# The list schedule of a transformer block's end: one shared interface for VectorE and GpSimd, subtractions dealt to either engine, new keys

## The chip, the cores and the metric

The kernel runs on one core of a Trainium2 chip. The metric is device time in microseconds for one launch. The kernel before takes 968.0 us (median of three runs, 967.63 to 968.37). Engines are named as in the profile: PE (TensorE matmuls), PEld (its weight loads), DVE (VectorE), ACT (ScalarE), POOL (GpSimd), SP (SyncE, which here issues the DMAs).

## The reference

One block with adaptive layer norm, sequence 2048, width 512, all in float32:

```python
mod = (_silu(c) @ w_mod).reshape(c.shape[0], 6, 1, -1)          # sa, ca, ga, sb, cb, gb
h = _layernorm(x) * (1 + ca) + sa
x = x + ga * A(h, wqkv, wo)      # 32 heads of 16, window of 256 keys, softmax, then @ wo
h = _layernorm(x) * (1 + cb) + sb
x = x + gb * ((_silu(h @ w1) * (h @ w3)) @ w2)                  # inner width 1792
```

## The kernel before, in words

**Arithmetic.** A float32 product is made of three PE products of halves: each operand is split into a high part (rounded to the PE's fp32r, by ACT) and a low part (operand minus high part, one TENSOR_TENSOR on DVE or POOL). So every operand costs an ACT copy and a subtraction with two inputs in SBUF; these subtractions are what the change is about.

**Stages.** First projections and layer norm 1. Then 32 units of attention, one per four heads and quarter of the sequence ("block" b = 0 to 3, 512 rows): scores (L485 for the row maxima, L752 for the probabilities), maxima on DVE (L494), masks on DVE (L760, L772), exponentials on ACT (L765, L767), products with the values into the bank `po` (L720), a copy `os` (L814) stored to `o_dr[b]` (L817). The rows of q and k go through `ringq` and `ringk` by DMA (L457, L459). The last units also hold nothing but their own work and what the end puts between.

**The end.** What follows the attention is one program of some thousand operations, and its first part is laid between the last units of attention. For each block: `o_sums` loads the softmax sums (L1065, tile `wqr` for the first 24 heads of a block, `mT` for the last 8), takes reciprocals on DVE (L1069) and stores them to `r_dr`; `o_part` loads four quarters k of the attention's output (L1089) and the spread reciprocals (L1084), multiplies them (L1101), and splits the result: high part on ACT (L1093), low part (L1096), into tiles `o` (blocks 0, 2, 3) or `x1b` (block 1). `o_proj` multiplies with `wo` (L1113, 48 matmuls a block, 12 per tile of 128 rows); `add_stats` adds the residual on DVE with a row sum (L982) and squares on ACT (L990); `ln_rstd` makes 1/sqrt on POOL (L1004) between two small DVE operations (L1001, L1007). `ln2` applies layer norm 2 to blocks 0 and 1 on ACT (L1233), transposes on PE (L1247), scales on ACT (L1251, tiles t0 to t3), and forms the operands of one level of Strassen's scheme: sums and differences (`sub`, L1264, tiles t1 to t5) and splits (`cut`, L1270 on ACT and L1272, tiles b000 to b611: operand, half k, part). `half_rows` does the layer norm of blocks 2 and 3 for later (L1299 on ACT, L1308 on PE, L1312). The FFN follows: 14 steps of 14 products `up` (L1375, six matmuls each), sums on DVE (L1406), gates, and 8 products `down` (L1468). Its weights are loaded (L1171, L1214) and split (`split`: L966 on ACT, L967 on POOL).

**What sets the order.** The operations of the end are recorded with engine, duration, priority (`key`), the tiles they read and write. `Sched.deal` walks in time: for each engine it takes the first ready operation in order of key that can start when the engine is free, and issues the earliest over all engines. The attention's remaining operations stand in `fixed` at given times and are merged in; they go first at equal time. Every engine runs its queue in this order, so an operation that waits for a tile holds all that stand behind it on its engine. Durations of the plan: a subtraction 0.85 on DVE or 1.29 on POOL, engines independent of each other. Which engine makes a product or subtraction is written out: in `K["by"]` for `o_part`, as an argument in `ln2` (`cut(B11, h11, "DVE")`, `sub(t3, h22, h12, "POOL")`), POOL for the weights. `K` also has the keys.

## Time and profile before

| | |
|---|---|
| median of three runs | 968.0 us (967.63 to 968.37) |
| the profiled execution's own time | 967.35 us |
| its span, first to last instruction | 965.6 us |
| mean granted clock | 0.988 |
| busy: PE, DVE, ACT, POOL | 921.7, 672.0, 524.8, 544.1 us |
| last product of the attention ends (L720) | 471.4 us after the span's start |
| last matmul of `o_proj` ends (L1113) | 532.9 us |

The span is 1.75 us shorter than that execution's own time, and the execution is 0.65 us under the median; the prediction makes its sum on the span and adds both. In the lines quoted below, a row of a timeline has start and duration in us, engine, line and operation, output<-inputs with shapes, how many are merged in the row, and in brackets the idle time before it and what ended it. A row of a table by stretches has the stretch, its length, busy time (and number of instructions) of PE, PEld, DVE, ACT and POOL, the granted clock of PE, the DMA engines' share and GB/s. A row of waits has who waited for whom, the total in us, how often, and the longest.

### The profile page before, as it was taken

How to read it: one execution, taken by the hardware profiler on the slowest of the kernel's cores; microseconds unless marked ns; L12 is line 12 of the kernel's file. 1: busy time of each engine (PE TensorE's matmuls, PEld its weight loads, DVE VectorE, ACT ScalarE, POOL GpSimd, SP SyncE). 2: the span in 40 equal slices, each digit the busy share in tenths (PEclk: the TensorE clock that was granted, in tenths of full speed). 3: DMA queues.
4: the chain of work that ended last, by engine and by line, in shares of the span. 5: the costliest groups of instructions: out<-in, count | busy, mean ns of one | idle time of the engine just before them, and what ended most of it. 6: DMA issues, size and time to landing. Idle time of an engine off the chain costs nothing.

```text
span 965.6 us, 16735 instructions
## 1 busy us (share of the span) xinstructions
PE 921.7 (95%) x5330; PEld 708.9 (73%) x5330; DVE 672.0 (70%) x1864; ACT 524.8 (54%) x1031; POOL 544.1 (56%) x691
## 2 busy tenths in 40 slices
PE   5999999999999999978987999999999999999998
PEld 2678677777777777755665878888888888888886
DVE  7575689898898989876568555675569645565455
ACT  3333677787877777764677654333455334433330
POOL 5221465676656665643665689986657446443420
PEclk9999999999999999998998999999999999999999
DMA  9532466656665665566870668654254512322002
GB/s 307 174 87 46 105 186 163 153 149 163 183 170 139 163 160 149 138 181 183 247 218 1 206 222 312 215 184 162 77 166 149 182 42 95 98 65 92 25 22 87
DMA packets 125020, 141.62 MB, mean 147 GB/s; under 512 B 60034, under 2 KB 72834, under 8 KB 124932
## 3 DMA queue, kind: packets, MB, share of 16 engines
q1 hardware_dynamic: 124212, 139.51, 49.3%
q10 hardware_dynamic: 720, 1.05, 0.3%
q8 instruction: 42, 0.69, 0.3%
q14 instruction: 46, 0.38, 0.1%
HBM read 85.72 MB, written 34.61 MB: 125 GB/s over the span
## 4 chain that ended last, share of the span: by engine, by line
PE 82%; DVE 7%; ACT 3%; DMA 3%; issue 3%; SPq 1%; POOL 1%; DVEq 0%; POOLq 0%; ACTq 0%
PE mx L1375 12%; PE st L1375 12%; PE pj L438 9%; PE st L752 8%; PE mx L485 8%; PE po L720 8%; PE st L1468 7%; PE mx L1468 7%; PE pj L1375 4%; PE st L652 2%; PE pj L1468 2%; PE st L1113 1%; PE mx L1113 1%; DVE junk L494 1%; DMA wo<-wsum 1%
## 5 line engine op out<-in xcount | busy, mean ns | idle before, releaser
L494 DVE CUSTOM_DVE_ANT_0 junk<-mx,mskq 128x320 bf16<-128x320 f32 (+4 forms) x512 | 223.0, 465 | 37.9 <-PE mx L485 37.1
L967 POOL TENSOR_TENSOR w<-w,w 128x512 fp32r<-128x512 f32 (+2 forms) x56 | 106.8, 1924 | 117.5 <-ACT w L966 99.0
L485 PE MATMUL mx<-ringk,ringq 96*128 96x320 f32 (+4 forms) x512 | 153.8, 324 | 5.5 <-DMA ringq<-qk 3.0
L752 PE MATMUL st<-ringq,ringk 98*128 98x256 f32 (+1 forms) x528 | 141.4, 336 | 7.1 <-DVE st L772 3.1
L779 POOL TENSOR_SCALAR_AFFINE_SELECT pt<-pt 128x256 f32<-128x256 f32 x224 | 92.4, 412 | 88.3 <-ACT pt L767 80.7
L438 PE MATMUL pj<-hT,wq 128*128 128x512 f32 x384 | 132.3, 402 | 1.8 <-ACT wq L423 1.0
L485 PEld LDWEIGHTS mx<-ringk,ringq 96*128 96x128 f32 x512 | 97.8, 192 | 44.5 <-DVE mt L494 21.4
L767 ACT ACTIVATE pt<-st 128x512 f32<-128x512 f32 (+1 forms) x198 | 115.8, 587 | 25.9 <-DVE st L760 7.7
L752 PEld LDWEIGHTS st<-ringq,ringk 98*128 98x128 f32 x528 | 91.1, 193 | 22.0 <-ACT pt L767 5.4
L720 PE MATMUL po<-pt,vS 128*17 128x384 f32 (+2 forms) x1408 | 92.5, 392 | 2.8 <-ACT pt L767 1.5
L438 PEld LDWEIGHTS pj<-hT,wq 128*128 128x128 f32 x384 | 68.3, 191 | 10.2 <-ACT wq L423 1.4
L1375 PE MATMUL mx<-b,w 128*128 128x512 f32 x264 | 68.2, 397 | 6.0 <-ACT t L1409 5.7
L1406 DVE TENSOR_TENSOR t<-mx,t 128x512 f32<-128x512 f32 x48 | 33.0, 689 | 45.3 <-PE mx L1375 22.6
L1406 DVE TENSOR_TENSOR t<-st,t 128x512 f32<-128x512 f32 x48 | 33.1, 690 | 44.7 <-PE st L1375 25.0
L720 PEld LDWEIGHTS po<-pt,vS 128*17 128x17 f32 x1408 | 34.8, 98 | 39.4 <-issue 19.9
L1375 PEld LDWEIGHTS mx<-b,w 128*128 128x128 f32 x264 | 50.1, 191 | 17.2 <-ACT t L1409 6.0
L1446 ACT ACTIVATE wq<-g 128x512 fp32r<-128x512 f32 x28 | 17.7, 631 | 81.6 <-DVE g L1402 33.6
L772 DVE COPY_PREDICATED st<-later,st 128x256 f32<-128x256 uint8 x112 | 47.4, 423 | 18.7 <-PE st L752 16.2
L1375 PE MATMUL st<-b,w 128*128 128x512 f32 x240 | 60.3, 390 | 0.0
L794 POOL TENSOR_SCALAR_AFFINE_SELECT sm<-sm 128x256 f32<-128x256 f32 x109 | 42.6, 409 | 28.7 <-ACT sm L784 27.7
L760 DVE TENSOR_TENSOR st<-st,mskr 128x256 f32<-128x256 f32 x125 | 53.6, 429 | 7.0 <-PE st L752 5.8
L451 POOL TENSOR_TENSOR qk<-qkr,qk 128x512 fp32r<-128x512 f32 x32 | 42.2, 1320 | 25.8 <-ACT qk L447 25.8
(262 smaller groups left out, 2020.7 us busy)
## 6 DMA issues: line engine op xcount, KB each, us to landing
ringk<-qk SPq DMA_DIRECT2D x96, 128.0 KB
ringq<-qk SPq DMA_DIRECT2D x192, 64.0 KB
o_dr<-os SPq DMA_DIRECT2D x32, 256.0 KB
w<-wsum SPq DMA_DIRECT2D x14, 512.0 KB
w<-w2g SPq DMA_DIRECT2D x14, 512.0 KB
jb<-in_w SPq DMA_DIRECT2D x24, 256.0 KB
wraw<-in_w SPq DMA_DIRECT2D x7, 768.0 KB
w<-wraw SPq DMA_DIRECT2D x14, 384.0 KB
```

The costliest lines, as they stand in the source:

```text
L438: nc.tensor.matmul(v["ps"], WQ[g][w][:, n // 3], hTp(i, n // 3, b * BT, BT), start=(n == 0), stop=(n == 3 * KC - 1))
L485: nc.tensor.matmul(v[i][:, :n], both_queries(a, gs), keys(NS, a, (gs + 1) * HP - n, n), start=True, stop=True)
L494: nc.vector.tensor_tensor_reduce(out=junk[:, :n], in0=v[i][:, :n], in1=mskq[:, WK - n:], scale=1.0, scalar=-3e38, op0=ALU.add, op1=ALU.max ...
L720: nc.tensor.matmul(po[32 * i:32 * i + DH + 1, qb * P:(qb + nq) * P], vS[:, kb, 4 * g + i], pts[i // 2][:, i % 2, c0:c0 + nq], start=first, ...
L752: nc.tensor.matmul(o, keys(NM, a, kb * P, P), queries(a, q, n), start=q == lo, stop=not plus and q + n == hi, skip_group_check=True)
L760: nc.vector.tensor_tensor(out=ps, in0=ps, in1=mskk[:, p:p + 1].to_broadcast([P, 2, P]), op=ALU.add)
L767: nc.scalar.activation(held[u, j, a][:, :, :n], v[j, a, 0].rearrange("p (h q) k -> p h q k", h=2)[:, :, :n], AF.Exp, scale=SCALE)
L779: nc.gpsimd.affine_select(out=pt[:, :, 2 * m], in_=pt[:, :, 0], **w)
L967: sch.op(eng, lambda: on_eng(eng).tensor_tensor(out=lo(), in0=src(), in1=hi().bitcast(F32), op=ALU.subtract), 0.06 + 0.0024 * n if eng == ...
L1375: nc.tensor.matmul(ps(bk), WT[s, n][w][:, col], BB[t, k][r], start=start and c == 0, stop=stop and c == 5, skip_group_check=True)
L1406: return nc.vector.tensor_add(o, x, y)
L1468: nc.tensor.matmul(ps(bk), tiles[hk + (h,)][:, i * P:(i + 1) * P], w2_of(last, y, f), start=(m == 0), stop=(m == 5))
```

## The change

`Sched.op` gets a flag `port`, and `deal` a time `port` until which the one interface is taken: an operation with two inputs in SBUF on DVE or POOL starts only when it is free. POOL's operations of the attention (`fixed`) take it too, DVE's do not. The low part in `o_part` and its multiplication, `sub` and `cut` in `ln2`, and weight splits with a key under `w0` + 13 are recorded for either engine (`both`); whichever would end earlier gets them, at 0.72 (DVE) or 1.32 (POOL) for 512 columns. All keys in `K` are new, and so is `n`, the number of quarters that must be there before the first product of a block's tile (1, 1, 2, 1 before, 2, 2, 3, 1 now). What is computed stays the same. The core of the diff:

```diff
-    def op(self, eng, fn, occ, key, reads=(), writes=(), lat=None, mode=0):
+    def op(self, eng, fn, occ, key, reads=(), writes=(), lat=None, mode=0, port=False):
+
+
         o = Op()
-        o.eng, o.fn, o.occ, o.key, o.mode = eng, fn, occ, key, mode
+        o.both = occ if isinstance(occ, dict) else None
+        if o.both:
+            eng, port, occ = "DVE", True, occ["DVE"]
+        o.eng, o.fn, o.occ, o.key, o.mode, o.port = eng, fn, occ, key, mode, port
...
-            insort(ready[o.eng], (o.key, o.seq, o))
+            for e in ("DVE", "POOL") if o.both else (o.eng,):
+                insort(ready[e], (o.key, o.seq, o))
...
-                    s = o.est
+                    s = max(o.est, port) if o.port else o.est
+                    if o.both:
+                        a, z = (max(s, free[x]) + o.both[x] for x in (e, "POOL" if e == "DVE" else "DVE"))
+                        if z < a:
+                            continue
...
+                if e == "POOL":
+                    port = max(port, free[e])
...
+            if o.both:
+                o.eng, o.occ = e, o.both[e]
+                o.lat = o.occ + HOP[e]
...
+            if o.port:
+                port = max(port, free[o.eng])
+            order.append((lambda fn=o.fn, e=o.eng: fn(e)) if o.both else o.fn)
...
-BY = ((("POOL", "POOL"),) * 3 + (("DVE", "DVE"),), (("POOL", "POOL"),) * 3 + (("DVE", "DVE"),),
-      (("POOL", "DVE"),) * 3 + (("DVE", "DVE"),), (("POOL", "POOL"),) * 4)
 K = dict(be=(('DVE', 'DVE'), ('DVE', 'POOL'), ('DVE', 'POOL'), ('POOL', 'POOL'), ('POOL', 'DVE'),
-         ('POOL', 'DVE'), ('DVE', 'DVE')), hr=0.109, de=7.098, wo=-0.159, x1=5.764, xb=-29.382,
-         xl=0.241, os=-0.129, ol=(-15.316, -4.484, -6.572, 4.956), pl=(3.999, 1.87, -4.828,
-         102.62), pe=(0.982, -5.962, 56.258, 232.622), o=(1.381, 8.497, 20.124, -0.531), n=(1, 1,
-         2, 1), w0=62.113, l2=0.424, f=1.543, fl=40.897, by=((('POOL', 'POOL'), ('DVE', 'DVE'),
-         ('DVE', 'POOL'), ('DVE', 'DVE')), (('DVE', 'DVE'), ('DVE', 'POOL'), ('DVE', 'DVE'),
-         ('DVE', 'POOL')), (('POOL', 'POOL'), ('POOL', 'DVE'), ('DVE', 'POOL'), ('POOL', 'DVE')),
-         (('POOL', 'DVE'), ('DVE', 'POOL'), ('DVE', 'POOL'), ('DVE', 'POOL'))), w=0.559, dn=1.412,
-         ds=0.003, l3=-0.027)
+         ('POOL', 'DVE'), ('DVE', 'DVE')), hr=-16.49, de=-4.33, wo=-4.756, x1=14.729, xb=-20.73, xl=16.783,
+         os=-10.171, ol=(-2.159, 0.83, 2.928, 0.264), pl=(8.637, 0.137, -19.926, 113.617), pe=(-7.191, -13.987,
+         57.285, 244.957), o=(-12.234, 1.729, 12.09, -3.422), n=(2, 2, 3, 1), w0=61.143, l2=4.34, f=14.693,
+         fl=45.503, w=10.173, dn=1.848, ds=0.034, l3=-21.35)
...
+    EITHER, ANYT = dict(DVE=0.72, POOL=1.32), K["w0"] + 13
...
+        if key < ANYT:
+            sch.op(None, lambda e: on_eng(e).tensor_tensor(
+                out=lo(), in0=src(), in1=hi().bitcast(F32), op=ALU.subtract),
+                   dict(DVE=0.08 + 0.00125 * n, POOL=0.06 + 0.0025 * n), key, kl + kh, kl)
+            return
         sch.op(eng, lambda: on_eng(eng).tensor_tensor(
             out=lo(), in0=src(), in1=hi().bitcast(F32), op=ALU.subtract),
-               0.06 + 0.0024 * n if eng == "POOL" else 0.85, key, kl + kh, kl)
+               0.06 + 0.0024 * n if eng == "POOL" else 0.85, key, kl + kh, kl, port=True)
...
-        sch.op("POOL", root, 1.0, key, sq, ["rs" + tag])
+        sch.op("POOL", root, 1.0, key, sq, ["rs" + tag], port=True)
...
-        by, minus = K["by"][b][k]
-        sch.op(by, lambda: on_eng(by).tensor_tensor(out=v["ot"], in0=v["ot"], in1=v["rt"], op=ALU.mult),
-               SPAN[by], key + 0.4, [on, rn], [on])
+        sch.op(None, lambda e: on_eng(e).tensor_tensor(out=v["ot"], in0=v["ot"], in1=v["rt"], op=ALU.mult),
+               EITHER, key + 0.4, [on, rn], [on])
         sch.op("ACT", hi, act(512) + 0.1, key + 0.4, [on], [(on_, 0, k)])
-        sch.op(minus, lo, SPAN[minus], key + 0.4, [on, (on_, 0, k)], [(on_, 1, k)])
+        sch.op(None, lo, EITHER, key + 0.4, [on, (on_, 0, k)], [(on_, 1, k)])
...
-                def go():
+                def go(e):
                     if o[0] not in tiles:
                         fresh(o[0], o[1], F32, (P, BT), "fp")
-                    (nc.gpsimd if eng == "POOL" else nc.vector).tensor_tensor(
-                        out=tiles[o[0]], in0=tiles[a[0]], in1=tiles[b[0]], op=ALU.subtract)
-                sch.op(eng, go, 1.29 if eng == "POOL" else 0.85, key, [a[1], b[1]], [o[1]])
+                    on_eng(e).tensor_tensor(out=tiles[o[0]], in0=tiles[a[0]], in1=tiles[b[0]], op=ALU.subtract)
+                sch.op(None, go, EITHER, key, [a[1], b[1]], [o[1]])
...
-                sch.op(eng, lambda: (nc.gpsimd if eng == "POOL" else nc.vector).tensor_tensor(
+                sch.op(None, lambda e: on_eng(e).tensor_tensor(
                     out=BB[m, k][1], in0=tiles[src[0]], in1=BB[m, k][0].bitcast(F32),
-                    op=ALU.subtract), 1.29 if eng == "POOL" else 0.85, key, [src[1], hi], [lo])
+                    op=ALU.subtract), EITHER, key, [src[1], hi], [lo])
```

Line numbers in the new kernel differ: `o_sums` loads at L1084 and takes reciprocals at L1088, `o_part` multiplies at L1117 and subtracts at L1113, the row sums are at L1001, `sub` and `cut` at L1280 and L1287, the weights' subtraction at L982 (either engine) or L986 (POOL), 1/sqrt at L1023.

**First place: the queue of SP, and DVE behind it, in the last units of attention** (about 418 us before, 53 us ahead of the attention's last product). `wqr<-o_dr` are loads of the softmax sums, `x1a<-in_x` of the residual, `wo<-wog` of the output weights, `ringq`, `ringk` the rows for the next unit's scores. SP before:

```order
L457 DMA ringk<-qk_7040 32x2x512
L1065 DMA wqr<-o_dr_71 96x1x128
L1050 DMA x1a<-in_x 128x512 x4
L1044 DMA wo_7148<-wog 128x512 x4
L1065 DMA wqr<-o_dr_72 96x1x128
L459 DMA ringq<-qk_7109 16x16x64 x2
L457 DMA ringk<-qk_7109 32x2x512
```

and now:

```order
L469 DMA ringk<-qk_7040 32x2x512
L1084 DMA wqr<-o_dr_71 96x1x128
L1084 DMA wqr<-o_dr_72 96x1x128
L1084 DMA wqr<-o_dr_73 96x1x128
L1084 DMA wqr<-o_dr_74 96x1x128
L1106 DMA wq_7160<-o_dr_71 128x1x512
L1069 DMA x1a<-in_x 128x512 x2
L1063 DMA wo_7148<-wog 128x512 x4
L1069 DMA x1a<-in_x 128x512 x2
L471 DMA ringq<-qk_7109 16x16x64 x2
L469 DMA ringk<-qk_7109 32x2x512
```

Two more loads of sums and one quarter of the attention's output now stand ahead of the rows. On DVE the four reciprocals of these sums stood singly, in four places of the last units; now one row holds them all, at the first of those places, ahead of a mask:

```order
L772 TENSOR_TENSOR st<-st,mskr 128x256
L1088 RECIPROCAL wqr<-wqr 96x128 x4
L784 COPY_PREDICATED st<-later,st 128x2x128
```

Later on DVE, where POOL had them or where they stood after the attention's maxima, three multiplications (L1117) and three subtractions (L1113) of block 0 now stand between the maxima of the last two units.

**Second place: DVE at the end of the attention** (about 461 to 472 us before). The masks L760 (now L772) are the last that the attention needs. Before:

```order
L1101 TENSOR_TENSOR qk_7615<-qk_7615,qk_7584 128x512
L1101 TENSOR_TENSOR wq_7419<-wq_7419,wq_7541 128x512
L760 TENSOR_TENSOR st<-st,mskr 128x2x128
L1096 TENSOR_TENSOR o_7150<-wq_7419,o_7149 128x512
L1069 RECIPROCAL mT<-mT 32x128
L1101 TENSOR_TENSOR wq_7716<-wq_7716,wq_7668 128x512
L760 TENSOR_TENSOR st<-st,mskr 128x2x128
L982 ISA x1a,nmB_7772<-pj,x1a 128x512
```

and now:

```order
L1088 RECIPROCAL mT<-mT 32x128
L772 TENSOR_TENSOR st<-st,mskr 128x2x128 x2
L1088 RECIPROCAL mT<-mT 32x128
L982 TENSOR_TENSOR wo_7148<-wo_7148,wo_7147 128x512
L1117 TENSOR_TENSOR wq_7428<-wq_7428,wq_7550 128x512
L1117 TENSOR_TENSOR qkr<-qkr,qk_7652 128x512
L1117 TENSOR_TENSOR qk_7722<-qk_7722,qk_7663 128x512
L1113 TENSOR_TENSOR o_7150<-wq_7428,o_7149 128x512
L1117 TENSOR_TENSOR wq_7732<-wq_7732,wq_7677 128x512
L1001 ISA x1a,nmB_7832<-pj,x1a 128x512
```

The two masks now stand together, with no multiplication between them. The fourth quarter of block 0 (`wq_7428`, before `wq_7419`) was multiplied and split ahead of the last mask and is now done behind it.

**Third place: the operands of the FFN** (about 504 to 526 us before). POOL before, from the weights' splits to the 1/sqrt of block 3:

```order
L967 TENSOR_TENSOR w21_7829<-w21_7829,w20_7828 128x512
L1264 TENSOR_TENSOR t4_8103<-t1_8076,t2_8089 128x512
L1272 TENSOR_TENSOR b201_7805<-t1_8076,b200_7804 128x512
L1272 TENSOR_TENSOR b501_7817<-t4_8103,b500_7816 128x512
L1264 TENSOR_TENSOR t4_8155<-t1_8140,t2_8147 128x512
L1272 TENSOR_TENSOR b211_7807<-t1_8140,b210_7806 128x512
L1272 TENSOR_TENSOR b511_7819<-t4_8155,b510_7818 128x512
L1096 TENSOR_TENSOR o1_7150<-wq01_7958,o0_7149 128x512
L1096 TENSOR_TENSOR o1_7150<-qk1_7886,o0_7149 128x512
L1096 TENSOR_TENSOR o1_7150<-wq00_7898,o0_7149 128x512
L1004 TENSOR_TENSOR rsB2_8049<-sqB2_8048,nhalf_65 128x4
```

Of these, POOL now has the weights' split and the 1/sqrt alone. On DVE there now stands, in one run from the first difference (t4 of half 0) to the second half's:

```order
L1280 TENSOR_TENSOR t4_8128<-t1_8106,t2_8114 128x512
L1280 TENSOR_TENSOR t2_8114<-t2_8114,t0_7999 128x512
L1280 TENSOR_TENSOR t5_8141<-t1_8106,t2_8114 128x512
L1287 TENSOR_TENSOR b501_7801<-t4_8128,b500_7800 128x512
L1287 TENSOR_TENSOR b101_7785<-t3_8126,b100_7784 128x512
L1287 TENSOR_TENSOR b401_7797<-t5_8141,b400_7796 128x512
L1287 TENSOR_TENSOR b301_7793<-t2_8114,b300_7792 128x512
L1280 TENSOR_TENSOR t5_8141<-t3_8126,t5_8141 128x512
L1287 TENSOR_TENSOR b201_7789<-t1_8106,b200_7788 128x512
L1287 TENSOR_TENSOR b011_7783<-t0_8150,b010_7782 128x512
L1287 TENSOR_TENSOR b601_7805<-t5_8141,b600_7804 128x512
L1280 TENSOR_TENSOR t4_8174<-t1_8169,t2_8164 128x512
```

Then t2, t5 and b111 follow, the last operand of the second product `up`: 15 subtractions on DVE with nothing else between. Before, DVE's queue held 13 operations from b101 to b111, two of them of another kind (an L1096 and an L982), while POOL had the six L1264 and L1272 shown above beside it. On PE one product changed its place there: the third product `up` (operand b4) now stands ahead of the last 36 matmuls of `o_proj`, where before the second was the last ahead of them. In the rest of the FFN the same products stand in nearly the same order, the products `down` behind the whole of the next 14 products `up` instead of among the last of them.

25 lines of the change are left out of this document (12 added, 13 removed).

## The prediction

> **What bounds the kernel now.** I read the page's busy times first, then the stretches of 20 us, then what PE waited for in the stretch where it is not full.
>
> ```profile
> span 965.6 us, 16735 instructions
> PE 921.7 (95%) x5330; PEld 708.9 (73%) x5330; DVE 672.0 (70%) x1864; ACT 524.8 (54%) x1031; POOL 544.1 (56%) x691
> ...
> 420.00:440.00 20.00, 14.49 (x93) 10.03 (x93) 12.54 (x42) 10.41 (x23) 10.35 (x15) 0.83 0.77 219
> 480.00:500.00 20.00, 16.73 (x74) 12.98 (x72) 15.87 (x29) 13.95 (x25) 16.66 (x10) 1.00 0.94 286
> 500.00:520.00 20.00, 12.74 (x58) 9.99 (x57) 15.18 (x20) 16.55 (x31) 11.35 (x8) 0.89 0.06 24
> 520.00:540.00 20.00, 18.98 (x78) 15.55 (x79) 10.55 (x24) 12.33 (x24) 5.74 (x5) 0.86 0.30 93
> 540.00:560.00 20.00, 20.00 (x96) 16.37 (x95) 13.84 (x15) 16.27 (x26) 19.05 (x14) 1.00 0.55 176
> sum 160.00, PE 137.31 PEld 103.51 DVE 101.90 ACT 100.54 POOL 97.96; mean PE 17.16 PEld 12.94 DVE 12.74 ACT 12.57 POOL 12.24
> ...
> PE mx L1375 <- ACT t L1409: 5.7, 1, 5.7
> PE st L752 <- DVE st L772: 2.9, 3, 2.0
> PE mx L485 <- DVE mt L494: 1.5, 1, 1.5
> PE mx L1308 <- ACT e L1312: 1.0, 1, 1.0
> ```
>
> PE is full 95% of the span. From 420 to 580 us (the sum row is of those eight stretches) it is busy 137.3 of 160 us, in several of them at a granted clock of 0.83 to 0.89; from 540 us on it is full but for one wait of 1.0. So the kernel is PE from end to end with 22.7 us of holes where attention hands over to the FFN, and the change, which moves only work of that handover, can win or lose there alone. PE's work is the same before and after. Below, T is the end of the attention's last L720 (471.4, the row of 470.98 under A).
>
> **The change part by part.**
>
> *D, the operands of the FFN: what the change is best at.* The rows are DVE's, POOL's, ACT's and PE's of the stretch of the longest hole.
>
> ```profile
> 506.00 0.69 DVE L1272 TENSOR_TENSOR b<-t,b 128x512 fp32r<-128x512 f32 x1 [4.57 <-ACT b L1270]
> 506.61 3.50 DVE L1264 TENSOR_TENSOR t<-t,t 128x512 f32<-128x512 f32 x2
> 513.34 3.13 DVE L1272 TENSOR_TENSOR b<-t,b 128x512 fp32r<-128x512 f32 x2
> 516.39 3.42 DVE L1264 TENSOR_TENSOR t<-t,t 128x512 f32<-128x512 f32 x2
> 519.74 4.04 DVE L1272 TENSOR_TENSOR b<-t,b 128x512 fp32r<-128x512 f32 x3
> ...
> 504.71 1.28 POOL L1264 TENSOR_TENSOR t<-t,t 128x512 f32<-128x512 f32 x1 [5.80 <-ACT t L1251]
> 514.19 3.40 POOL L1272 TENSOR_TENSOR b<-t,b 128x512 fp32r<-128x512 f32 x2
> 517.56 1.71 POOL L1096 TENSOR_TENSOR o<-wq,o 128x512 fp32r<-128x512 f32 x1
> ...
> 503.21 1.43 ACT L1251 ACTIVATE t<-st,modc 128x512 f32<-128x512 f32 x2
> 505.33 1.68 ACT L1270 ACTIVATE b<-t 128x512 fp32r<-128x512 f32 x3
> ...
> 521.01 2.93 PE L1375 MATMUL mx<-b,w 128*128 128x512 f32 x6 [5.68 <-ACT t L1409]
> ```
>
> A subtraction alone steps by 0.61 on DVE (506.00 to 506.61) and takes 1.28 on POOL. Beside each other both slow down: DVE 1.56 to 1.71 (3.13 and 3.42 for two), POOL 1.70. The two therefore yield a pair per 1.70 us, 0.85 an operation, while DVE alone yields one per 0.61, and each step of a chain is 1.1 us shorter on it. From ACT's first t1 (503.21) to the second product `up` (521.01) the stretch takes 17.8 us now. In the new order that product needs 15 subtractions on DVE (the third place shown above): 15 x 0.61 = 9.2. ACT then is the slower: ahead of b110's high part its queue has seven L1251 of 0.72, eight L1270 of 0.56 (rows above), one square, counted like an L1233 of 0.80, and one L1093 of 0.62 (both in the rows of term B): 5.0 + 4.5 + 0.8 + 0.6 = 10.9, then b111 itself and a handover, 0.9. That is 11.8, **-6.0**. Bounds: a chain that goes to and fro between ACT and DVE instead of streaming could add 3; the DVE rate alone would give 9.8, so -3 to -8.
>
> The Trainium skill ("SBUF — State Buffer", section "SBUF: two separate sides") calls this pair of ports an exclusive lock, held for a whole instruction while the other engine stands still. By that a pair would cost 0.69 + 1.28 = 1.97 and not the 1.70 of the rows; the measured rate decides, and with POOL's share gone the new stretch is the same by either. The rule also speaks against the change: it leaves POOL three weight splits (w11 and two of w21) just where DVE now does all the rest, and by a lock each would hold DVE for its whole length; ACT is busy there beyond them (term B), so the sum would not change.
>
> *A, the last units of attention.*
>
> ```profile
> 418.51 0.87 SPq L1065 DMA_DIRECT2D wqr<-o_dr  x1
> 424.78 1.34 SPq L459 DMA_DIRECT2D ringq<-qk  x2
> 428.07 1.69 SPq L1065 DMA_DIRECT2D wqr<-o_dr  x2
> 430.04 0.57 SPq L1089 DMA_DIRECT2D qkr<-o_dr  x1
> ...
> 425.48 5.17 DMA ringq<-qk
> ...
> 421.18 0.95 DVE L1069 RECIPROCAL wqr<-wqr 96x128 f32<-96x128 f32 x1 [1.71 <-DMA wqr<-o_dr]
> 469.47 0.69 DVE L1101 TENSOR_TENSOR wq<-wq,wq 128x512 f32<-128x512 f32 x1 [0.92 <-POOL o L1096]
> 470.08 0.43 DVE L760 TENSOR_TENSOR st<-st,mskr 128x256 f32<-128x256 f32 x1
> 470.98 0.41 PE L720 MATMUL po<-pt,vS 128*17 128x128 f32 x8 [1.46 <-ACT pt L767]
> ```
>
> Three more reciprocals ahead of the mask: it comes 3 x 0.9 = 2.7 later, and PE waits for it already (the L772 wait of 2.0). The rows for the next scores leave SP later by the two more loads (1.7) and the quarter of output (0.6), 2.3, with 256 KB more ahead of them in flight, 1.2 at the 219 GB/s of that stretch: up to 3.5. The two delays run side by side: +3.0. Against them: three reciprocals are gone from DVE later (2.7), six multiplications and subtractions of 0.61 are added among the maxima (3.7), where DVE was late for PE by 1.5 once (the L494 wait): +0.4. At the end the two last masks no longer stand behind a multiplication that waits for its tiles, so the wait of 1.46 goes, and of the earlier waits for masks about 1.0; three multiplications of block 1 now stand ahead of a mask: +0.9; -1.5 together. **A = +1.9**, bounds -1 (all of the first delay absorbed by what waits for the rows anyway) to +4 (every addition on the path).
>
> *B, from T to the first t1.* Loads and copies of the first weights, and the first applications of layer norm 2:
>
> ```profile
> 474.46 0.54 SPq L1171 DMA_DIRECT2D w<-wraw  x1
> 478.83 0.54 SPq L1214 DMA_DIRECT2D w<-w2g  x1
> ...
> 480.24 0.85 ACT L966 ACTIVATE w<-w 128x768 fp32r<-128x768 f32 x1 [0.46 <-DMA w<-wraw]
> 484.66 0.80 ACT L1233 ACTIVATE wqr<-x1a,nbB,rsB 128x512 f32<-128x512 f32 x1
> 507.62 0.62 ACT L1093 ACTIVATE o<-qkr 128x512 fp32r<-128x512 f32 x1
> ```
>
> PE has 117 matmuls of `o_proj` left at T, now as before (27 of block 0's 48 stand ahead of it in both orders); at 0.227 (the chain's row of 36 in 8.17, under E) that is 26.6. Two waits join it. The fourth quarter of block 0 now stands behind the last mask: a reciprocal of 0.9 and five operations of 0.61 from T - 1.0, done at T + 2.9, while PE wants it at T + 0.7: 2.2. And ACT takes all four weight copies and both of w2 ahead of the first L1233; a weight's load took 5.8 from issue to copy (474.46 to 480.24), w2's is issued at T + 7.4, later by the one delayed store, so ACT is through at about T + 16 and the fourth applied tile comes 4 to 5 later, where PE has come to want them at T + 18: 2. With 0.9 for eight transposes, at half a matmul each, PE is at T + 31.7 and ACT, after two high parts, begins t1 at T + 33.6. Before it was 503.21, T + 31.8. **B = +1.8**, bounds -2 (both waits hidden) to +4 (loads 2 us later still). DVE's last row sum of block 1, late today behind POOL's splits, comes earlier, which the queue of ACT hides.
>
> *E, the first products.* Two rows of the chain of waits; `x36` and `x6` are matmuls:
>
> ```profile
> 476.40 8.17 PE st L1113 x36
> ...
> 533.45 1.39 PE st L1375 x6
> ```
>
> From 521.01 to the end of the third product (533.45 + 1.39) PE takes 13.8, part of it at half the clock after the hole. In the new order the same three groups hold two products (1.4 to 2.9 each), 36 matmuls (8.2) and transposes (0.4): 13.1. **E = -0.7**, bounds 1 either way. *F, the later wait of 1.0*: the transposes L1308 that waited for e now all stand ahead of the first products `down`, so I take **-1.0**, bounds -1 and 0. The rest of the FFN I cost at nothing: PE covers it, POOL is at 19.05 of 20 and yet nobody waits for it; should its cover fail, a split of 128x1024 late by its own length would cost about 2.5.
>
> Sum: 1.9 + 1.8 - 6.0 - 0.7 - 1.0 = -4.0. The span becomes 961.6, with the 1.75 around it 963.35; that execution is 0.65 under the median, so **964.0 us**.
>
> **The rivals.** *Larger gain.* A and B come to nothing, because the delays at the first place fall into waits that PE has anyway and the weights land in time: -7.7 and up to 1 more, **about 959.5**. For it: 22.7 us of holes, and DVE only 12.54 of 20 busy at 420. Against it: PE waited for just those two things. *No change.* The gain of D is real but the FFN's first stage was to wait anyway, or A and B are at their upper parts, +6: -1.6 or less, **about 967.5**. *Slower.* DVE's queue becomes the attention's brake: an operation that waits for a DMA holds masks and maxima behind it, in three places (the multiplications between the maxima, the one ahead of the third last mask, the reciprocal `mT` ahead of block 0's last row sum). Price: 3 to 5 us each, as the loads of 5.17 and the wait of 1.71 above show. It decides once two of the three come late: 2 x 3.5 beyond A, B and D as above gives +3, **about 971.5**. For it: the DMA share of 0.77 to 0.94 in these stretches. Against it: the loads are issued earlier too. *The change does nothing*: excluded for the moves, which the new order shows; possible for the effect, counted with no change.
>
> **How the numbers follow.** A difference under 0.2% (1.9 us) can't be told from no change by this measurement. Chances: forecast (-1.9 to -6) 0.37, larger gain 0.21, no change 0.20, slower 0.22. So faster 0.58, same 0.20, slower 0.22. The time is that of the forecast, 964.0; its own range by the bounds of the terms is 961 to 967. The range for 8 in 10 takes in the larger gain with D at its bound (956.5) and the slower case (971.5).
>
> **What would show it.** D right: DVE's L1280 and L1287 at steps of 0.6 to 0.7 with POOL idle beside them, and 11 to 13 us from t1 to the second product `up`. A: the end of L720 at 472 to 474. B: a wait of about 2 for block 0's fourth quarter and one on the applied tiles. E, F: o_proj's end at about 529 and no wait of PE after it. The forecast is wrong if the attention ends after 476, if DVE's subtractions still take 1.5 or more each, or if PE waits for weights in the FFN.

## The result, and the profile after

The change makes the kernel slower: 976.7 us (median of nine runs, 972.8 to 982.9) against 968.4 us (967.6 to 971.8) for the kernel before on the same chip, ratio 1.0074 with a 95% interval of 1.0056 to 1.0092. The same kernel timed once more gave 1.0067 [1.0041, 1.0093]. The forecast was 964.0, its range 956.5 to 971.5.

The page of the kernel after, and what PE waited for from 420 us to the end. The profiled execution is its longest, so its 15.5 us over the span before overstate the loss.

```profile
span 981.1 us, 16716 instructions
PE 928.9 (95%) x5330; PEld 711.7 (73%) x5330; DVE 691.8 (71%) x1885; ACT 528.6 (54%) x1031; POOL 502.7 (51%) x670
...
PE st L764 <- DVE st L784: 4.8, 2, 4.5
PE mx L497 <- DVE mt L506: 3.9, 2, 2.1
PE st L1390 <- ACT t L1424: 3.9, 1, 3.9
PE mx L497 <- DMA r_dr<-wqr: 3.0, 1, 3.0
PE st L1390 <- DVE x1a L1488: 2.5, 2, 1.8
PE st L1129 <- ACT st L1009: 1.8, 1, 1.8
PE mx L1390 <- DVE t L1421: 1.8, 1, 1.8
```

The first, second and fourth rows lie in the attention, the third and sixth in the turn from attention to FFN. The fifth and seventh lie in the FFN, where the kernel before had one wait of 1.0. Three stages, each from its profile (start of the scores that wait 0.58 us for L765, now L777; end of the attention's last product; end of `o_proj`; end of the span):

| | attention's last units | turn | FFN |
|---|---|---|---|
| before | 51.5 | 61.6 | 432.6 |
| after, profiled execution | 58.1 | 60.4 | 440.3 |
| after, a second profile (of the run again) | 57.6 | 58.3 | 437.0 |

The new order has one product `up` more (six matmuls) in the turn. The row of before is on the short side in the attention: thirteen profiles of kernels whose attention has the order of before, the experiments' included, give 50.2 to 53.7 us there, median 52.7. So the change makes the attention some 5 us longer, and not quite the 6.1 to 6.6 of the table.

Next come the FFN's stretch of 410 us that starts at 545 us, and from its first 255 us (545 to 800) two groups of DVE's operations that read two operands in SBUF: gate times sum (L1402, now L1417) and the largest group of low parts of hidden units (L1449, now L1464). First the kernel before, one row by stretches and two by groups:

```profile
545.00:955.00 410.00, 408.97 (x1782) 332.24 (x1781) 245.44 (x334) 165.43 (x260) 243.76 (x184) 1.00 0.39 129
...
L1402 DVE TENSOR_TENSOR g<-t,g 128x512 f32<-128x512 f32 x27 | 26.4, 979 | 5.5 <-POOL t L1418 4.8
L1449 DVE TENSOR_TENSOR wq<-g,wq 128x512 fp32r<-128x512 f32 x18 | 15.4, 857 | 0.7 <-ACT wq L1446 0.7
```

and the same of the kernel after:

```profile
545.00:955.00 410.00, 403.43 (x1744) 325.63 (x1743) 258.57 (x323) 171.82 (x264) 235.88 (x181) 1.00 0.41 133
...
L1417 DVE TENSOR_TENSOR g<-t,g 128x512 f32<-128x512 f32 x24 | 35.5, 1494 | 5.4 <-POOL t L1433 4.8
L1464 DVE TENSOR_TENSOR wq<-g,wq 128x512 fp32r<-128x512 f32 x16 | 26.1, 1662 | 1.2 <-ACT wq L1461 1.2
```

PE is idle for 6.6 us of the 410 instead of 1.0, and DVE is busy 13 us longer with fewer operations. Up to 800 us its gate product takes 1.49 us instead of 0.98, its subtraction 1.66 instead of 0.86; over the whole 410 us these means are 1.16 instead of 0.88 and 1.52 instead of 0.80.

### The profile page after: what moved, and what is told of

It is laid out like the page before. It is cut to its first block, busy times and chain, and to the rows that moved or that the text cites. A ratio compares the mean times of both kernels' runs of the same rounds, so it can differ in the third digit from the quotient of the medians.

```text
span 981.1 us, 16716 instructions
## 1 busy us (share of the span) xinstructions
PE 928.9 (95%) x5330; PEld 711.7 (73%) x5330; DVE 691.8 (71%) x1885; ACT 528.6 (54%) x1031; POOL 502.7 (51%) x670
## 4 chain that ended last, share of the span: by engine, by line
PE 73%; DMA 7%; DVE 6%; ACT 4%; issue 3%; POOL 3%; SPq 3%; POOLq 0%; ACTq 0%; DVEq 0%
PE st L1390 10%; PE mx L1390 10%; PE pj L450 8%; PE st L764 8%; PE po L732 7%; PE mx L497 7%; PE mx L1483 6%; PE st L1483 6%; PE pj L1390 4%; PE st L664 2%; PE pj L1483 2%; PE mx L1129 1%; DMA w<-wsum 1%; DMA w<-w2g 1%; POOL e L888 1%
## 5 line engine op out<-in xcount | busy, mean ns | idle before, releaser
L764 PE MATMUL st<-ringq,ringk 98*128 98x256 f32 (+1 forms) x528 | 144.0, 341 | 11.6 <-DVE st L784 5.0
L986 POOL TENSOR_TENSOR w<-w,w 128x512 fp32r<-128x512 f32 (+2 forms) x53 | 91.5, 1740 | 105.8 <-ACT w L980 77.9
L1390 PE MATMUL st<-b,w 128*128 128x512 f32 x270 | 68.2, 397 | 7.0 <-ACT t L1424 3.9
L980 ACT ACTIVATE w<-w 128x512 fp32r<-128x512 f32 (+2 forms) x56 | 42.7, 787 | 57.7 <-DMA w<-w2g 21.8
L1421 DVE TENSOR_TENSOR t<-mx,t 128x512 f32<-128x512 f32 x43 | 29.6, 689 | 51.6 <-PE mx L1390 42.4
L1390 PEld LDWEIGHTS st<-b,w 128*128 128x128 f32 x270 | 51.0, 191 | 19.2 <-ACT t L1424 4.4
L772 DVE TENSOR_TENSOR st<-st,mskr 128x256 f32<-128x256 f32 x125 | 53.5, 428 | 10.8 <-PE st L764 9.8
L1390 PE MATMUL mx<-b,w 128*128 128x512 f32 x240 | 60.7, 396 | 0.0
```

Of the source, the lines that this page charges most:

```text
L764: nc.tensor.matmul(o, keys(NM, a, kb * P, P), queries(a, q, n), start=q == lo, stop=not plus and q + n == hi, skip_group_check=True)
L772: nc.vector.tensor_tensor(out=ps, in0=ps, in1=mskk[:, p:p + 1].to_broadcast([P, 2, P]), op=ALU.add)
L986: sch.op(eng, lambda: on_eng(eng).tensor_tensor(out=lo(), in0=src(), in1=hi().bitcast(F32), op=ALU.subtract), 0.06 + 0.0024 * n if eng == ...
L1390: nc.tensor.matmul(ps(bk), WT[s, n][w][:, col], BB[t, k][r], start=start and c == 0, stop=stop and c == 5, skip_group_check=True)
L1421: return nc.vector.tensor_add(o, x, y)
```

## The experiments

Both kernels record the same 1629 operations of the end and differ in the order in which `deal` issues them, and on which engine. Most experiments therefore replace the choice in `deal` by a table of (operation, engine), which reproduces either kernel's order exactly and lets one part of one order be joined to the rest of the other:

```diff
-            best = None
-            for e, lst in ready.items():
-                ...
+            n = ORDER.pop(0)
+            o = self.ops[n // 2]
+            e = ("DVE", "POOL")[n % 2] if o.both else o.eng
```

Their line numbers are those of the kernel after. Each ratio is to the kernel before on the same chip; the runs were made on several chips, on which the kernel before had medians of 968.4 to 971.2 us, so a gain or loss in us is the ratio's unless a sentence speaks of medians. What was expected of each run stands in the order of the list above it.

**Which stage loses.**

```diff
 again:     the kernel after, as it is
 new_ffn:   attention, turn: order of before;          FFN: order of the change
 new_front: attention, turn: order of the change;      FFN: order of before
 new_turn:  attention, FFN: order of before;           turn: order of the change
```

> The changed kernel once more, for a second profile: the first one was its longest execution (982.9 us where the median is 976.7). Expected 973 to 979 us. If the two losses read from the first profile are the kernel's own, they are here again: 3 to 6.5 us more than before between the first wait of the last units and the end of the attention, and 3 to 8 us of waits of PE in the FFN behind o_proj. If the FFN's waits were an accident of that execution, PE does not wait there, and the 6 us between the two executions lie in the FFN.

> The order of before up to the last product of o_proj, and from there the order of the change. Theory of two losses (the attention's end by its queues, the FFN by its own order, in which DVE has hidden-unit subtractions ahead of the additions that free PE's banks): 3 to 8 us slower than before, with waits of PE for L1488 and L1421 as in the profile of the change. Rival (one loss: the FFN's waits come only from a front that is late): within 1 us of before, and PE waits for neither.

> The order of the change up to the last product of o_proj, and from there the order of before. Two losses: the attention's +6.6 of the first profile less 2.7 gained from there to o_proj's end, so 2 to 5 us slower than before. One loss: all of it, 7 to 10 us slower. By the prediction as it was made (A +1.9, B to E -4.9): 3 us faster.

> The order of before to the end of the attention, then that of the change to the last product of o_proj, then that of before again. Here only the terms B, D and E act, without the delays of the attention: the prediction has -4.9 us for them (about 963.5), the first profile of the change -2.7 at equal work of PE (about 965.5). Rival: the gain is only a wait moved, and the FFN's first stage waits for weights instead: within 1 us of before.

| | median us | ratio |
|---|---|---|
| again | 975.2 | 1.0067 [1.0041, 1.0093] |
| new_ffn | 975.6 | 1.0067 [1.0043, 1.0091] |
| new_front | 969.6 | 1.0004 [0.9983, 1.0024] |
| new_turn | 966.5 | 0.9974 [0.9958, 0.9989] |

The FFN's order alone costs the whole +6.5 us (6.1 by the medians). Attention and turn together cost nothing, where 2 to 5 us were expected, and the turn alone gains 2.5 us (3.1 by the medians), which the new order of the attention takes away again. So the loss sits in the stage that the prediction had put at nothing. What PE waited for there, in new_ffn, a timeline of PE, then of DVE and of POOL just before the first of these waits:

```profile
565.45 2.27 PE L1390 MATMUL mx<-b,wo 128*128 128x512 f32 x6 [2.00 <-DVE t L1421]
...
654.95 3.02 PE L1390 MATMUL st<-b,w 128*128 128x512 f32 x12 [1.57 <-DVE x1a L1488]
...
753.28 0.50 PE L1390 MATMUL st<-b,wo 128*128 128x512 f32 x1 [1.37 <-DVE b L986]
...
558.20 2.90 DVE L1464 TENSOR_TENSOR qk<-g,qk 128x512 fp32r<-128x512 f32 x1
561.02 2.32 DVE L1464 TENSOR_TENSOR wq<-g,wq 128x512 fp32r<-128x512 f32 x1
...
555.88 6.91 POOL L986 TENSOR_TENSOR w<-w,w 128x768 fp32r<-128x768 f32 x3
```

PE waits three times, each time for DVE. Ahead of the first wait two subtractions take 2.90 and 2.32 us, beside three weight splits of 2.3 us on POOL. Behind that wait PE is slower for 6 us as well; by stretches (the granted clock is the third number from the end):

```profile
565.00:567.00 2.00, 1.55 (x5) 1.31 (x6) 1.09 (x2) 0.20 (x1) 1.52 (x2) 0.82 0.91 282
567.00:569.00 2.00, 2.00 (x8) 1.60 (x8) 0.69 (x1) 2.00 (x4) 1.84 (x4) 0.50 0.51 194
569.00:571.00 2.00, 2.00 (x9) 1.58 (x8) 0.00 (x0) 0.60 (x2) 2.00 (x2) 0.83 0.73 245
```

Three products and four transposes take 6.3 us there (565.45 to 571.77), where the same work takes 4.6 before (563.11 to 567.75): 1.7 us more. Behind the other two waits the clock stays at 1.00.

**Which part of the FFN's order.** `dn` and `ds` are the keys of the products `down`; dn_only is the kernel before with these two keys new (its line numbers are those of before):

```diff
-         (('POOL', 'DVE'), ('DVE', 'POOL'), ('DVE', 'POOL'), ('DVE', 'POOL'))), w=0.559, dn=1.412,
-         ds=0.003, l3=-0.027)
+         (('POOL', 'DVE'), ('DVE', 'POOL'), ('DVE', 'POOL'), ('DVE', 'POOL'))), w=0.559, dn=1.848,
+         ds=0.034, l3=-0.027)
```

ffn_but_dn has the change's FFN with these two keys as before. The other four start from new_ffn:

```diff
 adds_first:  in each step the 8 additions L1488 on DVE stand ahead of the 4 subtractions L1464
 splits_pool: the two weight splits of the second step that went to DVE (L982) are on POOL again
 jobs_after:  seven of POOL's sums L888, ahead of the splits of w, stand behind them
 jobs_adds:   jobs_after and adds_first
```

> The kernel before with two keys of the change alone (dn, ds): its attention and its turn to the FFN are word for word as before, and each stage's eight products down stand behind all 14 products up of the next stage instead of among the last of them. Theory 'place of the products down' (on DVE the hidden units' subtractions, L1449, then come ready together with the additions that free PE's banks and stand ahead of them): most of the 6.5 us that the whole new order of the FFN costs, so +3 to +6 us. Rival 'weight splits' (the splits that the change deals to DVE and moves on POOL collide with DVE's subtractions, whatever the place of the products down): within 1 us of before.

> The order of before up to the last product of o_proj, then the change's order of the FFN planned with the old dn and ds: its weight splits, loads and half_rows stand as the change has them, the products down as before. Place of the products down: the wait for L1421 at 565 us stays (2.0 and a slower clock behind it), the wait for x1a is gone, +1 to +3 us. Weight splits: +4 to +6.5 us.

> The kernel with the change's FFN alone (new_ffn, 975.6), with DVE's queue altered in one respect: in every stage the eight additions L1488 stand together ahead of the four subtractions L1464 that stood among and behind them. If the subtractions ahead of the additions are what costs, the wait for x1a goes and the time falls by 1.5 to 4 us. If not, it stays within 1 us of 975.6.

> The kernel with the change's FFN alone (new_ffn, 975.6) with two operations on another engine: the two weight splits of the second stage that the change deals to DVE (128x768 and 128x1024, 3.2 us together on DVE) are POOL's again, in the same place of the order. If they are what makes DVE late at the FFN's second stage, PE's wait of 2.0 for L1421 and the slower clock behind it go: 2 to 3.5 us faster than new_ffn. If it is the three splits on POOL that then run beside DVE's subtractions, the wait stays: within 1 us.

> The kernel with the change's FFN alone (new_ffn, 975.6), with one thing moved: seven short sums L888 on POOL, which stood ahead of the second stage's three weight splits L986, stand behind them (as before the change), so that the splits start some 3.5 us earlier and no longer run beside DVE's three subtractions L1464. If that coincidence is what makes DVE late at 565 us, those subtractions fall from 2.3 to 2.9 us to under 1, PE's wait of 2.0 for L1421 goes, and the time falls by 2 to 3.5 us. If the coincidence only moves to other operations of DVE, within 1 us.

> Both repairs of the change's FFN together (the sums behind the splits, and the additions ahead of the subtractions). If these two are the whole mechanism, PE is left with the wait of 1.4 for the second half's operands alone and the time is 0 to 2.5 us over before. If it stays 4 us or more over before, part of the cause is still unnamed.

| | median us | ratio |
|---|---|---|
| dn_only | 972.1 | 1.0027 [1.0008, 1.0047] |
| ffn_but_dn | 975.2 | 1.0052 [1.0035, 1.0070] |
| adds_first | 974.5 | 1.0041 [1.0022, 1.0059] |
| splits_pool | 977.6 | 1.0076 [1.0055, 1.0096] |
| jobs_after | 978.0 | 1.0062 [1.0045, 1.0080] |
| jobs_adds | 976.3 | 1.0058 [1.0039, 1.0076] |

The two keys alone cost 2.6 us and everything else alone 5.0. Each interval reaches about 2 us to either side, so neither their sum of 7.6 nor the 5.0 alone can be told from the 6.5 of both together: most of the loss is there without the two keys, and the two keys have a smaller one of their own. Of the repairs, adds_first alone may have won something (1.0 us by the differences of the medians, 2.5 by the ratios; its interval overlaps that of new_ffn); the others won nothing, though jobs_after did just what it was made for. The timeline of DVE and PE in jobs_after:

```profile
560.18 0.94 DVE L1464 TENSOR_TENSOR wq<-g,wq 128x512 fp32r<-128x512 f32 x1
...
624.91 1.67 PE L1390 MATMUL st<-b,wo 128*128 128x512 f32 x6 [1.43 <-DVE x1a L1488]
```

The slow subtraction is down to 0.94 us and the wait at 565 us is gone, but PE now waits at 625 us and three times more for the additions x1a. POOL has no fewer splits to do, and it may be that they now meet other operations of DVE; the next pair asks that question.

**Is it POOL's splits, or the order of the queues?** In both orders POOL's subtraction of each FFN weight was replaced by a fill with zeros; these two kernels leave the low parts of those weights out of the products. light_before has the order of before throughout, light_ffn that of new_ffn.

```diff
-        sch.op(eng, lambda: on_eng(eng).tensor_tensor(
+        sch.op(eng, lambda: on_eng(eng).memset(lo().bitcast(F32), 0.0) if eng == "POOL" else on_eng(eng).tensor_tensor(
             out=lo(), in0=src(), in1=hi().bitcast(F32), op=ALU.subtract),
```

> The order of before, complete; the subtraction of each FFN weight split that GpSimd does is replaced by a fill with zeros (so the low parts of those weights are left out of the products). If GpSimd's splits cost the FFN nothing in this order, the time is that of before, 968 to 970 us, PE full through the FFN; DVE's hidden-unit subtractions (L1464) fall from 0.86 us to about 0.7. If they cost something even here, it gains up to 1 us, the only wait there is.

> The same fill with zeros in the kernel that has the order of before up to o_proj and the order of the change in the FFN (new_ffn). Theory one, the loss of 6.5 us comes from GpSimd's splits beside DVE's operations (L1464 of 1.41 us, L1417 of 1.39 us there, against 0.86 and 0.98 in before's order): L1464 and L1417 fall to about 0.7 us, the three waits of 2.0, 1.6 and 1.4 us go, and the time is within 1 us of light_before. Theory two, the loss is in the order of DVE's and ACT's queues itself, whatever the operations last: 4 to 6 us above light_before, with waits for t L1421 and x1a L1488 left.

Measured: light_before 964.0 us, ratio 0.9949 [0.9928, 0.9970]; light_ffn 966.0, 0.9967 [0.9948, 0.9986]. The stretch of 410 us, of light_before:

```profile
545.00:955.00 410.00, 410.00 (x1789) 333.44 (x1788) 226.79 (x335) 167.58 (x261) 139.73 (x184) 1.00 0.40 129
```

and of light_ffn, with the groups from 545 to 800 us:

```profile
545.00:955.00 410.00, 410.00 (x1787) 333.51 (x1786) 222.38 (x335) 168.87 (x261) 135.36 (x178) 1.00 0.40 129
...
L1417 DVE TENSOR_TENSOR g<-t,g 128x512 f32<-128x512 f32 x27 | 18.5, 703 | 1.6 <-POOL t L1433 0.8
L1464 DVE TENSOR_TENSOR wq<-g,wq 128x512 fp32r<-128x512 f32 x18 | 13.4, 777 | 2.5 <-ACT wq L1461 2.5
L986 POOL MEMSET w<- 128x512 f32 (+2 forms) x34 | 24.1, 715 | 74.3 <-ACT w L980 61.7 <-PE st L1390 8.9 <-PE mx L1390 1.9
```

With the splits gone PE is busy for every one of the 410 us in either order, the FFN takes 431.3 us in both profiles (432.6 in that of the kernel before, 439.3 in that of new_ffn), and DVE's operations last 0.70 and 0.78 us (1.39 and 1.41 in new_ffn). The difference between the orders falls from 6.5 to 2.0 us in the medians (the two intervals overlap) and to nothing in the profiles. Theory one wanted less than 1 us and theory two 4 to 6 with waits left; the waits, all gone, decide for the first. The loss comes from POOL's splits meeting DVE's queue in the new order, but for the up to 2 us that the medians leave open. Two things are not told apart: a fill also ends 1.2 us earlier than a split of 1.88, so lateness of POOL itself went as well (though in new_ffn PE's waits all end with DVE); and of the 5 us that light_before gains, its FFN explains 1.3 in the profiles. These can't place the rest: the profiled execution of light_before is 2.5 us above its median, that of the kernel before 2.7 below its median on this chip.

**The attention.** The change puts the four reciprocals of the softmax sums together ahead of a mask, and work of block 0 among the maxima.

```diff
 recips_row:   before; on DVE the reciprocals of blocks 1 to 3 directly behind block 0's
               (on SP the loads of blocks 2 and 3 directly behind block 1's, all three behind x1a and wo)
 recips_first: before; the four loads first on SP, as in the change, the four reciprocals in a row
 no_hold:      new_front; the reciprocal mT and three multiplications L1117 behind the maxima
 turn_free:    new_turn; the four reciprocals behind the masks and maxima
```

> The order of before with one thing moved: the reciprocals of blocks 1 to 3 stand right behind that of block 0 on DVE, as the change has them, and their three loads behind the first on SP. By the prediction's first term the mask is 2.7 us later and PE's wait of 2.0 for it becomes about 4.7, the later places of the three give nothing back to PE except the 1.5 wait for maxima, so the end of the attention comes 1.5 to 3 us later. Rival (the delay is absorbed by the wait for the ring's rows behind it): the end of the attention within 0.7 us. In time: +1 to +3 by the first, within 1 by the second.

> The order of before with the four loads of sums first on SP, as the change has them, and their four reciprocals in a row on DVE ahead of the mask. The prediction's first term: the wait for the mask grows from 2.0 to about 4.5, the attention ends 1.5 to 3 us later, the time is 0.5 to 3 us over before. Rival (the reciprocals cost little and the change's other moves in the attention cost the rest): the end of the attention within 1 us of before.

> The kernel with the change's order up to o_proj's end (new_front, 969.6), with four operations moved on DVE: the reciprocal mT and the three multiplications that wait for loads stand behind the maxima of their unit instead of among them. If DVE's queue is the brake there, PE's two waits for maxima (1.85 and 2.10, in the second profile 2.8 together) go and the attention ends 2 to 4 us earlier; the time falls by 1 to 4. If the loads of the rows set the pace, the waits move to the next maxima and the time stays within 1.

> The fastest so far (new_turn, 966.5) with the same idea applied to the old attention: the four reciprocals that stand ahead of a mask or of maxima on DVE (wqr of blocks 0, 1 and 2, and one mT) stand behind them. PE's waits of 2.0 for the mask and of 1.5 for maxima go: the attention ends 2 to 3.5 us earlier and the time falls by 1 to 3.5 us, to 963 to 965.5. Rival (the gain is taken back by what waits for the stores of the reciprocals, or by the weights' loads after the attention): within 1 us of 966.5.

| | median us | ratio | attention, profile |
|---|---|---|---|
| recips_row | 973.8 | 1.0040 [1.0020, 1.0060] | 59.7 us |
| recips_first | 971.7 | 1.0009 [0.9991, 1.0026] | 53.9 us |
| no_hold | 971.1 | 1.0013 [0.9996, 1.0030] | 56.5 us |
| turn_free | 966.5 | 0.9969 [0.9951, 0.9987] | 52.0 us |

In recips_row the three loads thus do not stand right behind block 0's, as was expected of it; recips_first has them there. The wait for the mask in recips_row:

```profile
432.43 0.58 PE L764 MATMUL st<-ringq,ringk 98*128 98x256 f32 x1 [13.22 <-DVE st L784]
```

DVE stands idle for 8.6 us before block 1's reciprocal, whose load is behind others on SP, and with the three reciprocals PE waits 13.2 us for the mask behind them; at the attention's end 7 us of it are left (59.7 against the median of 52.7), in the time 3.9. With the loads issued first the mask waits 4.5 us, but neither the attention (53.9 us, against 50.2 to 53.7 with the order of before) nor the time is clearly longer. no_hold took away both waits for maxima, turn_free the wait for the mask, and neither gained. What stood there then, no_hold's PE first, then turn_free's:

```profile
432.64 0.60 PE L497 MATMUL mx<-ringk,ringq 96*128 96x320 f32 x1 [3.79 <-DMA r_dr<-wqr]
447.16 0.58 PE L764 MATMUL st<-ringq,ringk 98*128 98x256 f32 x1 [3.33 <-ACT pt L779]
```

```profile
429.86 0.62 PE L732 MATMUL po<-pt,vS 128*17 128x128 f32 x4 [3.02 <-ACT pt L810]
```

The wait of 3.33 is new. The other two had been there, shorter: 2.86 in new_front, 1.76 in new_turn. So the four reciprocals alone do not make the attention's 5 us, nor do the waits for maxima alone, and which of the other moves does is open.

**The turn.**

```diff
 subs_only: before; the six subtractions of ln2 that POOL had (L1280, L1287) on DVE
 fill:      new_turn; block 3's second and third quarters (L1110, L1113) on ACT and DVE right behind
            its first; the last 36 matmuls of o_proj ahead of and between the first two
            products up; the copy L1424 one place up on ACT
```

> The order of before in every place, with the six subtractions of layer norm 2 that POOL had now on DVE (term D alone; nothing else moves). By the prediction DVE then yields one subtraction per 0.61 and not a pair per 1.70: the 17.8 us from the first t1 to the second product shrink to about 12 to 14, and the time falls by 3 to 6 us. Rival: in the old order DVE's single queue delays the next operand as much as POOL did, or the products wait for weights: within 1.5 us of before.

> new_turn (966.5) with block 3's second and third quarters (two L1110 on ACT and two L1113 on DVE) right behind its first, o_proj's last 36 matmuls ahead of and between the first two products up instead of behind the third, and the copy L1424 one place up on ACT. If what is left of the hole is only that PE has nothing to do while ACT and DVE make the operands, the waits of 1.8, 0.9 and 4.0 us go and the time falls by 3 to 7 us, to 959.5 to 963.5. Rival (the FFN's next products then wait for their operands or banks in their turn): within 1.5 us of 966.5.

subs_only: 968.2 us, 0.9989 [0.9974, 1.0004]; by itself the step to DVE can't be told from nothing, and from the first t1 to the second product it takes 16.7 us, not the 12 to 14 expected. So what new_turn gained needs the new order as well. fill: **962.9 us, 0.9922 [0.9896, 0.9947]**, faster than both kernels. It rests on what new_turn still waits for at the second product `up`:

```profile
521.23 2.93 PE L1390 MATMUL st<-b,w 128*128 128x512 f32 x6 [3.97 <-ACT t L1424]
```

PE had 36 matmuls of `o_proj` behind this product, ready but for the two quarters' low parts. In fill they run in the hole: PE has 24 of them ahead of the first product and 12 between the first two, and neither of these two waits:

```profile
514.50 2.88 PE L1129 MATMUL st<-wo,o 128*128 128x512 f32 x12
517.22 1.53 PE L1390 MATMUL mx<-b,w 128*128 128x512 f32 x6
518.59 2.92 PE L1129 MATMUL st<-wo,o 128*128 128x512 f32 x12
521.35 2.89 PE L1390 MATMUL mx<-b,w 128*128 128x512 f32 x12
```

## Why the prediction was wrong

The step that failed is the sentence at the end of E and F: "The rest of the FFN I cost at nothing: PE covers it, POOL is at 19.05 of 20 and yet nobody waits for it; should its cover fail, a split of 128x1024 late by its own length would cost about 2.5." The cover did fail, though not by a late split. POOL's splits slow DVE's operations from 0.70 us to 1.4 and more, and in the new order the slowed gate products and subtractions hold, on DVE's queue, the sums and additions that PE needs next. In new_ffn's profile PE is idle 3.9 us longer over the 410 us than before, and its matmuls take 230.8 ns a record instead of 229.5 (405.05 us for 1755 records against 408.97 for 1782), 2.3 us more, of which 1.7 are the lower clock behind the first wait: 6.2 of the 6.7 us by which its FFN is longer (439.3 against 432.6). Rows that spoke for this stood in the profile before: DVE's two operations at 0.98 and 0.86 us, above those of 0.69 elsewhere, and a smaller group of the same subtractions (`qk<-g,qkr`) at 1.26, which takes 0.69 in light_before. And "the products `down` behind the whole of the next 14" was described ahead of the prediction as nearly the same order; the two keys that move them cost 2.6 us by themselves (dn_only).

The description ahead also says that an operation with two inputs in SBUF starts, in the plan, only when the interface is free. The code sets that flag for `o_part`, `ln2`, the layer norm and the weight splits, but not for DVE's L1417 and L1464. In the FFN the plan therefore never sees the meeting that costs the time.

By its other steps:

- **A** (+1.9, bounds -1 to +4): the attention took about 5 us longer (57.6 to 58.1 in the three profiles that have the change's order, new_front's 57.7 among them, against the median of 52.7), beyond the upper bound. The mask's delay was as reckoned (+2.5 against 2.7). Mis-sized was what follows it: the wait for the rows came to 3.0 where 1.5 had been, and two waits for maxima to 1.85 and 2.10, where one of 1.5 had been (+2.4 against the working's +0.4). From 417 to 482 us PE's waits are 13.5 to 14.5 us in these three profiles, and 9.3 to 10.6 in seven with the order of before. What is left of the 5 us is no wait: from 440 to 460 us the granted clock is 0.73 to 0.82 there, against 0.83 to 0.91. The end came at 480.5 us (476.9 in the second profile), over the 476 at which the forecast was to be wrong.
- **B** (+1.8): from the attention's end to the first t1 took 33.7 us in new_turn (507.51 less 473.80) against 31.8, +1.9; in the kernel after 32.9, +1.1. The size came out, the two waits behind it did not, so part of that is luck. PE waits for nothing of block 0's fourth quarter (2.2 in the working), only 0.3 (new_turn) and 0.8 (after) for a low part of block 1; for applied tiles it waits 2.3 and 1.5 in all. Behind the last of these the granted clock is 0.63 and 0.78 in new_turn (495.3 to 498 and to 501.2 us), where the working took full speed. The wait of 1.8 for ACT's squares (L1009) lies behind t1 and was in no term.
- **D** (-6.0): DVE's subtractions do step by 0.7 with POOL idle, as these rows of the kernel after show, DVE then ACT then PE, from the first t1 to the second product:

```profile
514.88 2.14 DVE L1280 TENSOR_TENSOR t<-t,t 128x512 f32<-128x512 f32 x3
516.94 2.65 DVE L1287 TENSOR_TENSOR b<-t,b 128x512 fp32r<-128x512 f32 x4
...
522.70 2.14 DVE L1280 TENSOR_TENSOR t<-t,t 128x512 f32<-128x512 f32 x3
524.76 2.64 DVE L1287 TENSOR_TENSOR b<-t,b 128x512 fp32r<-128x512 f32 x4
...
513.41 0.77 ACT L1267 ACTIVATE t<-st,modc 128x512 f32<-128x512 f32 x1
526.50 0.57 ACT L1424 ACTIVATE t<-st 128x512 f32<-128x512 f32 x1
...
527.13 2.92 PE L1390 MATMUL st<-b,w 128*128 128x512 f32 x6 [3.93 <-ACT t L1424]
```

  527.13 less 513.41 is 13.7, against 17.8 before: -4.1. The operand itself came as reckoned: the 15th subtraction is the first of the four from 524.76, done at about 525.4, 12.0 us after t1, where the working had 11.8. Late behind it is ACT's copy L1424 (done at 527.07), which stands behind high parts on its queue and was no part of the working.
- **E** (-0.7): from the second product to the end of the same work 13.7 against 13.8, -0.1. B, D and E together are -2.3 in place of -4.9; new_turn measured -2.5.
- **F** (-1.0): wrong in sign, since the FFN has more waits, not none. One of them, 1.16 us at 755 us, ends with a weight's high part on ACT in the profiled execution, which was a sign of being wrong too (in the second profile the wait at this place ends with DVE).
- **The range**: its lower end doesn't follow from its own terms, since 959.5 with D at -8 in place of -6 is 957.5, not 956.5.

Of the rivals, the slower one had the right sign and the wrong cause. What it named is in the trace: a multiplication waits 0.74 us and a reciprocal 1.19 for their loads, and maxima stand behind them; at the other two places a multiplication waits 2.85 and the reciprocal `mT` 3.33, of which PE feels 0.3 and 0.8. But it does not decide, as no_hold shows. A's terms were added to the turn's as if they lay one behind the other. In fact part of a delay in the attention comes back in the turn: with the change's attention ahead of it, the new turn took 58.3, 58.5 and 60.4 us, and with the attention of before 61.2 (new_turn); the attention's stage is 5.5 us longer in new_front than in new_turn, the median time 3.1. The likely reason, not tested, is that the loads and splits for the turn go on while PE waits.

The cited lock of the two ports ("SBUF — State Buffer", section "SBUF: two separate sides" in the Trainium skill) was rightly said to change nothing in the turn; I did not carry it into the FFN. By it, as an estimate, a subtraction of 0.70 us that starts with a split of 2.30 would last up to 3.0, and the trace agrees there with its 2.90. The same section says that such an operation of DVE meets only operations of GpSimd that read SBUF; the fills with zeros agree with it (0.70 and 0.78 us beside them).

## What to carry to other kernels

Before an order is changed over a stage that is "covered", look for operations there that already last longer than the same operations elsewhere: the stretching can be that of a shared resource, and a new order can put its price on the path. When a shared resource is added to a planner, all its users should be in it; no run here planned with the flag on L1417 and L1464, so what that would gain is open. And a hole of PE was closed better by work that is ready and stands behind it in PE's queue (fill, -0.78%) than by making the late operands a little earlier (new_turn, -0.26%, which fill contains), though fill also moved two quarters and a copy.

## What the runs showed of the hardware

- The stretching of one DVE operation can be nearly as long as a whole split of POOL: 2.90 us instead of 0.70 beside splits of 128x768 that take 2.30. Beside the shorter subtractions of the turn it was 1.70.
- The granted clock fell behind some waits of PE in the FFN and not behind others of the same length: to 0.50 behind the 2.00 us in new_ffn, but it stayed at 1.00 behind 1.76 in the second profile of the kernel after and behind 2.46 in splits_pool. What decides is not shown.
- Taking one wait away often only made another longer: five repairs (no_hold, turn_free, splits_pool, jobs_after, jobs_adds) won nothing that can be measured.
- The moment at which the compared stages begin varied between profiles from 418.0 to 422.4 us, in work that no kernel changed. The length of a stage varies too: with the order of before in it, the attention took 50.2 to 53.7 us and the turn 60.2 to 63.0. A difference of 2 us between two single profiles therefore says little; medians of several executions say more.
